# One decode step of attention and MLP on one core: wo in five chunks, buffers on lines of 512 bytes, eight unread matmuls

## The chip, the cores and the metric

The kernel runs on one core of one Trainium2 chip. Its time is device microseconds of one execution, as the median over several runs; the profile is one further execution, recorded by the hardware profiler. Of the core, the text speaks of PE (TensorE, the matmuls; PEld is its weight load), DVE (VectorE), ACT (ScalarE), POOL (GpSimd), SP (the queue that issues most transfers) and the 16 DMA engines that carry them. SBUF is the on-chip memory of 128 partitions, PSUM the accumulators that PE writes.

## The reference

One token goes through two branches that are added to it: attention over the last 4,096 positions of a cache with 4 key/value heads for 32 query heads, and a two-layer MLP. All arrays are bfloat16; D = 1024, F = 3584, head size 128.

```
xn = layernorm(x)
q  = (xn @ wq)                          # 1024 x 4096, 32 heads of 128
s  = q . k_cache[:, -4096:] / sqrt(128) # 4 heads, each for 8 query heads
o  = softmax(s) . v_cache[:, -4096:]
a  = o @ wo                             # 4096 x 1024
h  = gelu(layernorm(xn) @ w1 + b1)      # 1024 x 3584
b  = h @ w2 + b2                        # 3584 x 1024
out = x + a + b
```

## The kernel before

Everything that is computed is a product of one row with a large matrix, so nearly all of the 39.85 MB read are weights and cache, each used once. SP issues them in one queue, in this order: wq in four chunks, K of heads 0 and 1, W1 in three chunks, K of heads 2 and 3, V of four heads, W2 in two chunks, wo in seven chunks. A chunk is a number of rows of 128 partitions' worth: one row of wq is 8 KB per partition, of W1 7 KB, of W2 and wo 2 KB (`WQ_CHUNKS`, `W1_CHUNKS`, `W2_CHUNKS`, `WO_CHUNKS`, lines 22 to 25). Each chunk has a semaphore that its landing raises.

SBUF has three large buffers, allocated one behind the other after the small ones: KV (64 KB per partition, K and V), W1 (56 KB) and WA (64 KB). WA holds wq and later W2; W1 later holds wo rows 0 to 27; the K part of KV later holds wo rows 28 to 31 (`WOX`) and the output row (`OUT`). Hence three waits in SP's queue: W2 is issued once wq is used up (`pe_q`), wo once W1 is used up (`pe_h`), and the wo rows that lie in KV once the scores are done (`pe_sc`, line 426).

PE works in program order. First the sums of the layer norm of x (`pe_sum1`, line 286) and of xn (`pe_sum2`, line 312), each a matmul with a matrix of ones, followed by small DVE steps in `moments` (line 253). Then a loop over the 8 rows of wq (line 336), the spreading of q over heads (line 355), a loop over the 8 rows of W1 (line 389), a loop over 4 K heads (line 406), for which DVE transposes each K head as it lands (`turn_k`, line 345). Then the maximum, the exponentials and their transpose for the softmax, 32 matmuls with V (line 505), 56 with W2 (line 538) and 62 with wo (lines 549 and 558). The W2 and wo products go to two accumulators, `ACC[0]` for output columns 0 to 511 and `ACC[1]` for 512 to 1023, which lie in different rows of two PSUM banks. In the wo loop PE waits for each chunk's semaphore, then does two matmuls for each of its rows; the last chunk's pair stands in a block of its own, `pe_last`, which is branched to.

At the end ACT copies `ACC[0]` and DVE `ACC[1]` to SBUF. ACT issues the transfer of its half itself; SP waits for DVE and issues the other.

At the start POOL fills constants: identity matrices, ones, selection masks, zeros for `XZ`, `YZ` and `LQ`. DVE derives `SELI`, `QMASK`, `REPL` and `SEL2` from the identities between its layer-norm steps. `XZ` and `YZ` are zero but for the normalized x and y in every 97th column; PE reads shifted windows of them as its stationary operand.

Of the kernel before, what the change touches and what calls it, by code (L numbers as in the profile page):

```python
# [4 lines left out]
dt = mybir.dt  # L5
ALU = mybir.AluOpType
ACTF = mybir.ActivationFunctionType
AX = mybir.AxisListType

D = 1024  # L10
# [8 lines left out]
FC = F // 128  # L19
KC = D // 128  # L20
NQ = HQ * DH
WQ_CHUNKS = [1, 3, 2, 2]
W1_CHUNKS = [4, 2, 2]
W2_CHUNKS = [14, 14]
WO_CHUNKS = [13, 9, 4, 2, 2, 1, 1]

# [19 lines left out]
def bass_parallel_sum__sliding_block_cached__mixer_channel_mlp__decode_kernel(  # L46
# [17 lines left out]
    INV_D = 1.0 / D  # L64
# [3 lines left out]
    pe, dve, act, pool, sp = nc.tensor, nc.vector, nc.scalar, nc.gpsimd, nc.sync  # L68
# [12 lines left out]
    s_out = [nc.alloc_semaphore(f"s_out{n}") for n in range(2)]  # L81

    PE = Track(nc, "S_PE")
    DVE = Track(nc, "S_DVE")
    ACT = Track(nc, "S_ACT")
    POOL = Track(nc, "S_POOL")

    def sb(name, shape, dtype):
        return nc.alloc_sbuf_tensor(name, shape, dtype)

    identb = sb("identb", [128, 128], dt.bfloat16)
    identf = sb("identf", [128, 128], dt.float32)
    onesf = sb("onesf", [128, 128], dt.float32)
    SELI = sb("SELI", [128, 32], dt.float32)
# [6 lines left out]
    SEL2 = sb("SEL2", [4, 2], dt.bfloat16)  # L101
    XTT = sb("XTT", [128, 256], dt.bfloat16)
    XT16 = sb("XT16", [128, 16], dt.float32)
    msx = sb("msx", [128, 8], dt.float32)
    XNT = sb("XNT", [128, 8], dt.float32)
    XNTb = sb("XNTb", [128, 8], dt.bfloat16)
    YT16 = sb("YT16", [128, 16], dt.float32)
    msy = sb("msy", [128, 8], dt.float32)
    EXPW = sb("EXPW", [128, 1], dt.float32)
    YTb = sb("YTb", [128, 8], dt.bfloat16)  # L110
    TT = sb("TT", [128, 1024], dt.float32)
    QMASK = sb("QMASK", [128, 4], dt.float32)
# [11 lines left out]
    XZ = PT[:, 0:9 * 97 - 1]  # L124
    YZ = sb("YZ", [128, 9 * 97 - 1], dt.bfloat16)
    SELB = sb("SELB", [8, 2 * 97], dt.bfloat16)
    SUMP = sb("SUMP", [128, 1], dt.float32)
# [4 lines left out]
    OH = sb("OH", [32, DH], dt.bfloat16)  # L132
    OP = sb("OP", [128, 32], dt.bfloat16)
    KV = sb("KV", [128, HKV * W + HKV * NBLK * DH], dt.bfloat16)
    KT = KV[:, 0:HKV * W]
    WOX = KV[:, 0:4 * D]
    OUT = KV[0:33, 4 * D:4 * D + 512]
    V = KV[:, HKV * W: HKV * W + HKV * NBLK * DH]
# [34 lines left out]
    r = 0  # L173
# [12 lines left out]
    def ahead_of_barrier(engine, n):  # L186
# [15 lines left out]
    act.dma_start(XB[2:4, :], b2_rows).then_inc(s_b2, 16)  # L202
    DVE.mark(dve.memset(PS[:, 0:4 * 512], 0.0))

# [5 lines left out]
        base=0, channel_multiplier=1))  # L210
    c_onesf = POOL.mark(pool.memset(onesf[:, :], 1.0))
    POOL.mark(pool.memset(identb[:, :], 0.0))
    pool.wait_ge(POOL.sem, POOL.cnt)
    c_identb = POOL.mark(pool.affine_select(
        out=identb[:, :], in_=identb[:, :],
        pattern=[[-1, 128]], compare_op=ALU.not_equal, fill=1.0,
        base=0, channel_multiplier=1))
    POOL.mark(pool.memset(SEL[:, :], 0.0))
    pool.wait_ge(POOL.sem, POOL.cnt)
# [18 lines left out]
        out=SELB[:, :].rearrange("r (n m) -> r n m", n=2), in_=SELB[:, :].rearrange("r (n m) -> r n m", n=2),  # L238
        pattern=[[-16, 2], [-1, 97]], compare_op=ALU.not_equal, fill=1.0, base=0, channel_multiplier=16))
    POOL.mark(pool.memset(XZ[:, :], 0.0))  # L240
    c_z = POOL.mark(pool.memset(YZ[:, :], 0.0))
# [8 lines left out]
    def dve_dep():  # L250
        dve.wait_ge(DVE.sem, DVE.cnt)

    def moments(ms, T16):

        n = DVE.mark(dve.tensor_reduce(
            out=ms[:, 0:2],
            in_=PS[:, 7 * 512: 7 * 512 + 16].rearrange("p (a k) -> p a k", a=2),
            axis=AX.X, op=ALU.add))
        dve_dep()
        DVE.mark(dve.tensor_scalar(out=ms[:, 2:4], in0=ms[:, 0:2],  # L260
                                   scalar1=INV_D, scalar2=None, op0=ALU.mult))
        dve_dep()
        DVE.mark(dve.tensor_tensor(out=ms[:, 4:5], in0=ms[:, 2:3], in1=ms[:, 2:3], op=ALU.mult))
        dve_dep()
        v = DVE.mark(dve.scalar_tensor_tensor(
            out=ms[:, 5:6], in0=ms[:, 3:4], scalar=EPS, in1=ms[:, 4:5],
            op0=ALU.add, op1=ALU.subtract))
        act.wait_ge(DVE.sem, v)
        a = ACT.mark(act.activation(out=ms[:, 6:7], in_=ms[:, 5:6], func=ACTF.Sqrt))
        dve.wait_ge(ACT.sem, a)  # L270
        DVE.mark(dve.reciprocal(out=ms[:, 7:8], in_=ms[:, 6:7]))
        dve_dep()
        return n
# [10 lines left out]
    pe.wait_ge(DVE.sem, d_xsq)  # L284
    pe.wait_ge(POOL.sem, c_onesf)
    pe_sum1 = PE.mark(pe.matmul(PS[:, 7 * 512: 7 * 512 + 16], lhsT=onesf[:, :], rhs=XT16[:, 0:16]))  # L286
    dve.wait_ge(POOL.sem, c_identf)
    DVE.mark(dve.tensor_reduce(out=SELI[:, :], in_=identf[:, :].rearrange("p (i c) -> p c i", i=4),
                               axis=AX.X, op=ALU.add))
    dve_dep()  # L290
    DVE.mark(dve.tensor_reduce(out=QMASK[:, :], in_=identf[:, :].rearrange("p (t c) -> p t c", t=4),
                               axis=AX.X, op=ALU.add))
    DVE.mark(dve.tensor_copy(REPL[:, :].rearrange("p (i c) -> p i c", i=4),
                                      SELI[:, :].unsqueeze(1).to_broadcast([128, 4, 32])))
    dve.wait_ge(POOL.sem, c_identb)
    DVE.mark(dve.tensor_tensor(out=SEL2[:, :], in0=identb[0:4, 0:2], in1=identb[0:4, 2:4], op=ALU.add))
    dve.wait_ge(PE.sem, pe_sum1)
    moments(msx, XT16)
    DVE.mark(dve.tensor_scalar(out=XNT[:, :], in0=XT16[:, 0:8],
                               scalar1=msx[:, 2:3], scalar2=msx[:, 7:8],  # L300
                               op0=ALU.subtract, op1=ALU.mult))
    dve_dep()
    d_xn = DVE.mark(dve.tensor_copy(XNTb[:, :], XNT[:, :]))
    dve_dep()
    dve.wait_ge(POOL.sem, c_z)
    d_xz = DVE.mark(dve.tensor_copy(XZ[:, 96:9 * 97 - 1:97], XNTb[:, :]))
    DVE.mark(dve.tensor_copy(YT16[:, 0:8], XNTb[:, :]))
    dve_dep()
    d_ysq = DVE.mark(dve.tensor_tensor(  # L309
        out=YT16[:, 8:16], in0=YT16[:, 0:8], in1=YT16[:, 0:8], op=ALU.mult))  # L310
    pe.wait_ge(DVE.sem, d_ysq)
    pe_sum2 = PE.mark(pe.matmul(PS[:, 7 * 512: 7 * 512 + 16], lhsT=onesf[:, :], rhs=YT16[:, 0:16]))  # L312
    dve.wait_ge(PE.sem, pe_sum2)
    moments(msy, YT16)
    act.wait_ge(ACT.sem, ACT.cnt)
    ACT.mark(act.activation(out=EXPW[:, 0:1], in_=msy[:, 6:7], func=ACTF.Exp))
    d_y = DVE.mark(dve.tensor_scalar(
        out=YTb[:, :], in0=YT16[:, 0:8], scalar1=msy[:, 2:3], scalar2=msy[:, 7:8],
        op0=ALU.subtract, op1=ALU.mult))
    dve_dep()  # L320
    d_yz = DVE.mark(dve.tensor_copy(YZ[:, 96:9 * 97 - 1:97], YTb[:, :]))
    d_zs = DVE.mark(dve.memset(PS[:, 4 * 512:6 * 512], 0.0))

# [33 lines left out]
    dve.wait_ge(PE.sem, pe_qx)  # L357
    dve.wait_ge(POOL.sem, c_lq)
    act.wait_ge(PE.sem, pe_qx)
# [38 lines left out]

    pe.wait_ge(DVE.sem, d_zs)
    k_blocks = KT.rearrange("p (g n b j a) -> p g n b j a", g=HKV, n=2, b=16, j=4, a=32)  # L400
# [19 lines left out]
    def wo_at(r, nr):  # L420
        return W1[:, r * D:(r + nr) * D] if r < FC else WOX[:, (r - FC) * D:(r - FC + nr) * D]

    j0 = 0
    for j, nj in enumerate(WO_CHUNKS):
        if j0 == FC:
            sp.wait_ge(PE.sem, pe_sc)
        sp.dma_start(wo_at(j0, nj), wo_pm[:, j0 * D:(j0 + nj) * D]).then_inc(s_wo[j], 16)  # L427
        j0 += nj
# [17 lines left out]
    pe_nmb = PE.mark(pe.matmul(  # L446
        PS[:, 7 * 512 + 128: 7 * 512 + 129], lhsT=MX4[0:1, :], rhs=onesf[0:1, 0:1]))
    dve.wait_ge(PE.sem, pe_nmb)
# [33 lines left out]

    pe.wait_ge(s_b2, 32)
    pe.wait_ge(DVE.sem, d_nmb)
    for n in range(2):
# [7 lines left out]
    dve_dep()  # L493
    dve.wait_ge(POOL.sem, c_mask)
    DVE.mark(dve.tensor_scalar(out=RM[:, :], in0=MASK[:, :], scalar1=REC[:, 0:1], scalar2=None, op0=ALU.mult))
# [49 lines left out]
    for j, nj in enumerate(WO_CHUNKS[:-1]):  # L545
        pe.wait_ge(s_wo[j], 16)
        for _ in range(nj):
            for n in range(2):
                pe.matmul(ACC[n], lhsT=OP[:, r:r + 1], rhs=wo_at(r, 1)[:, n * 512:(n + 1) * 512],  # L549
                          start=False, stop=False)  # L550
            r += 1
    with nc.body("pe_turn", valid_engines=TENSOR):
        pe.br("pe_last").branch_hint(hint)
# [16 lines left out]
    a_out = ACT.mark(act.activation(out=OUT[0:1, :], in_=ACC[0], func=ACTF.Copy))  # L570
    act.wait_ge(ACT.sem, a_out)
    act.dma_start(out_row[:, 0:512], OUT[0:1, :]).then_inc(s_out[0], 16)
    sp.wait_ge(DVE.sem, d_out)
    sp.dma_start(out_row[:, 512:1024], OUT[32:33, :]).then_inc(s_out[1], 16)
    act.wait_ge(s_out[0], 16)
    sp.wait_ge(s_out[1], 16)

# [29 lines left out]
```

## Time and profile before

| | |
|---|---|
| median of 9 runs | 99.38 us (99.29 to 99.58) |
| the profiled execution's own time | 99.36 us |
| its span | 98.1 us |
| PE busy | 68.2 us, 69% of the span |
| DVE busy | 37.1 us, 38% |
| ACT, POOL busy | 5.8 and 6.7 us |
| granted PE clock, mean | 0.896 |
| DMA | 39.89 MB, mean 407 GB/s |
| packets on SP's queue (q1) | 3,458 |

The page cuts the span into 40 equal slices of 2.45 us. A digit is the busy share in tenths, 9 for 90% or more; PEclk is the clock granted to PE in the same tenths. The chain lists what ended last, followed back from the last instruction. In groups and timelines a line gives start, duration, engine, source line, operation and operands; in brackets stands the idle time before it and what ended it. A row of busy time by stretch gives the stretch, its length, then busy microseconds and count of PE, PEld, DVE, ACT and POOL, then PE's clock, the DMA share and GB/s.

### The profile page before, as it was taken

To read this page: it belongs to the slowest core of one execution; us is meant where nothing else is said; L and a number is where in the kernel's file an instruction comes from. 1 tells how busy PE (TensorE), PEld (TensorE's weight loads), DVE (VectorE), ACT (ScalarE), POOL (GpSimd) and SP (SyncE) were. 2 spreads that over 40 slices of the span, in tenths; PEclk is the share of its full clock that TensorE was granted. 3 is DMA by queue.
4 is the path that set the end of the run, shared out by engine and by line. 5 is a ranking of instruction groups with operands and counts; after the bars stand their busy time and mean duration, and the time that the engine had idled before them with its cause. 6 is when DMAs were issued, how large, how long until landed. Compare 5 with 4: busy or idle time off the path is not lost.

```text
span 98.1 us, 1063 instructions
## 1 busy us (share of the span) xinstructions
PE 68.2 (69%) x330; PEld 32.3 (33%) x330; DVE 37.1 (38%) x57; ACT 5.8 (6%) x11; POOL 6.7 (7%) x19
## 2 busy tenths in 40 slices
PE   0002299999983049999999743199991999754991
PEld 0002255555541025666644311133431233211320
DVE  4308571000018999500999544970008000000002
ACT  0500060000002000000000004000000000000002
POOL 6893000000000000000000000000000000000000
PEclk9999999999999556999999999755899589997599
DMA  5999999999999999999999999989989998989950
GB/s 154 434 483 453 392 434 434 427 391 428 438 526 397 386 403 427 444 402 428 428 428 428 428 446 514 409 374 514 421 374 469 416 445 377 458 385 420 413 226 8
DMA packets 3494, 39.89 MB, mean 407 GB/s; under 512 B 402, under 2 KB 420, under 8 KB 932
## 3 DMA queue, kind: packets, MB, share of 16 engines
q1 hardware_dynamic: 3458, 39.85, 95.8%
q8 instruction: 1, 0.02, 0.1%
q10 hardware_dynamic: 34, 0.01, 0.1%
q14 instruction: 1, 0.01, 0.0%
HBM read 39.86 MB, written 0.00 MB: 406 GB/s over the span
## 4 chain that ended last, share of the span: by engine, by line
DMA 81%; DVE 10%; SPq 4%; PE 2%; issue 1%
DMA KV<-in_A_k_cache_dram 43%; DMA KV<-in_A_wo_dram 38%; DVE KV L345 9%; PE PS L406 2%; SPq L176 1%; SPq L160 1%; SPq L166 1%; SPq L427 1%; DVE KV L568 1%; PE PS L558 0%
## 5 line engine op out<-in xcount | busy, mean ns | idle before, releaser
L345 DVE STREAM_TRANSPOSE KV<-KV 128x4096 bf16<-128x4096 bf16 x4 | 17.5, 4424 | 6.0 <-DMA KV<-in_A_k_cache_dram 5.9
L336 PE MATMUL PS<-WA,PT 128*97 x64 | 16.8, 433 | 0.1
L389 PE MATMUL PS<-W,YZ 128*97 x64 | 13.8, 379 | 4.2 <-POOLq L248 4.2
L389 PEld LDWEIGHTS PS<-W,YZ 128*97 x64 | 8.5, 133 | 9.4 <-issue 5.9
L336 PEld LDWEIGHTS PS<-WA,PT 128*97 x64 | 9.1, 143 | 7.4 <-issue 2.8
L549 PE MATMUL PS<-W,OP 128*1 128x512 bf16 x56 | 8.1, 452 | 3.0 <-DMA W<-in_A_wo_dram 3.0
L505 PE MATMUL PS<-KV,PT 128*32 128x512 bf16 x32 | 9.8, 481 | 0.1
L568 DVE CAST KV<-PS 1x512 bf16<-1x512 f32 x1 | 0.7, 683 | 20.1 <-PE PS L558 20.1
L538 PE MATMUL PS<-WA,GT 128*1 128x512 bf16 x56 | 7.9, 452 | 0.0
L406 PE MATMUL PS<-KV,LQ 128*128 x32 | 7.2, 380 | 0.5 <-DVE KV L345 0.5
L348 DVE STREAM_TRANSPOSE TT<-PS 128x1024 f32<-128x1024 f32 x1 | 1.2, 1250 | 14.1 <-PE PS L336 14.1
L286 PE MATMUL PS<-XT,onesf 128*128 128x16 f32 x2 | 0.6, 386 | 8.5 <-DVE XT L282 8.5
L505 PEld LDWEIGHTS PS<-KV,PT 128*32 128x32 bf16 x32 | 3.7, 117 | 5.8 <-issue 3.8
L549 PEld LDWEIGHTS PS<-W,OP 128*1 128x1 bf16 x56 | 2.7, 96 | 8.3 <-issue 3.5
L406 PEld LDWEIGHTS PS<-KV,LQ 128*128 x32 | 3.1, 98 | 4.5 <-issue 1.6
L538 PEld LDWEIGHTS PS<-WA,GT 128*1 128x1 bf16 x56 | 2.7, 96 | 4.7 <-issue 2.3
L510 DVE TENSOR_TENSOR TT<-PS,RM 32x512 f32<-32x512 f32 x1 | 0.7, 678 | 7.1 <-PE PS L505 7.1
L286 PEld LDWEIGHTS PS<-XT,onesf 128*128 128x128 f32 x2 | 0.5, 313 | 8.5 <-DVE XT L282 8.5
L452 ACT ACTIVATE Pe<-PS,NMB 128x512 bf16<-128x512 f32 x2 | 1.3, 683 | 28.4 <-DVE NMB L449 28.4
L570 ACT ACTIVATE KV<-PS 1x512 bf16<-1x512 f32 x1 | 0.6, 586 | 30.8 <-PE PS L558 30.8
L312 PE MATMUL PS<-YT,onesf 128*128 128x16 f32 x2 | 0.6, 384 | 2.4 <-DVE YT L309 2.4
L277 DVE STREAM_TRANSPOSE XTT<-XR 128x256 bf16<-128x256 bf16 x1 | 0.6, 631 | 4.2 <-DMA XR<-in_A_x_dram 4.2
(92 smaller groups left out, 33.7 us busy)
## 6 DMA issues: line engine op xcount, KB each, us to landing
WA<-in_B_w_dram SPq DMA_DIRECT2D x2, 3584.0 KB, 40.6
WA<-in_A_wq_dram SPq DMA_DIRECT2D x2, 2048.0 KB, 17.9
KV<-in_A_k_cache_dram SPq DMA_DIRECT2D x4, 1024.0 KB, 32.8
KV<-in_A_v_cache_dram SPq DMA_DIRECT2D x4, 1024.0 KB, 37.1
W<-in_B_w_dram SPq DMA_DIRECT2D x1, 3584.0 KB, 32.3
W<-in_B_w_dram SPq DMA_DIRECT2D x2, 1792.0 KB, 37.9
W<-in_A_wo_dram SPq DMA_DIRECT2D x1, 3328.0 KB, 34.5
WA<-in_A_wq_dram SPq DMA_DIRECT2D x1, 3072.0 KB, 11.2
```

The costliest lines, as they stand in the source:

```text
L160: sp.dma_start(WA[:, a:b], wq_pm[:, a:b]).then_inc(s_wq[j], 16)
L286: pe_sum1 = PE.mark(pe.matmul(PS[:, 7 * 512: 7 * 512 + 16], lhsT=onesf[:, :], rhs=XT16[:, 0:16]))
L336: last = pe.matmul(PS[0:97, n * 512:(n + 1) * 512], lhsT=shifted(XZ, s)[:, bass.ds(k, 1), :], rhs=wq_rows[:, bass.ds(k, 1), s * 1024 + n * ...
L345: dve.transpose(out=KT[:, g * W:(g + 1) * W], in_=KT[:, g * W:(g + 1) * W]).then_inc(r_k, 1)
L348: DVE.mark(dve.transpose(out=TT[:, :], in_=PS[:, 0:1024]))
L389: last = pe.matmul(PS[0:97, (2 + n) * 512:(2 + n) * 512 + HW], lhsT=shifted(YZ, s)[:, bass.ds(k, 1), :], rhs=w1_rows[:, bass.ds(k, 1), c: ...
L406: last = pe.matmul(PS[:, (4 + n) * 512:(5 + n) * 512], lhsT=q_blocks[:, bass.ds(g, 1), j, :], rhs=k_blocks[:, bass.ds(g, 1), n, :, j, :], ...
L452: a_exp = ACT.mark(act.activation(out=Pe[:, n * 512:(n + 1) * 512], in_=PS[:, (4 + n) * 512:(5 + n) * 512], func=ACTF.Exp, scale=SCALE, bi ...
L505: last = pe.matmul(PS[0:32, 0:512].rearrange("p (g d) -> p g d", g=HKV), lhsT=PT[:, b * 32:(b + 1) * 32], rhs=Vb[:, b, :, :], start=(b == ...
L538: pe.matmul(ACC[n], lhsT=GT[:, c:c + 1], rhs=W2[:, c * D + n * 512: c * D + (n + 1) * 512], start=False, stop=False)
L549: pe.matmul(ACC[n], lhsT=OP[:, r:r + 1], rhs=wo_at(r, 1)[:, n * 512:(n + 1) * 512], start=False, stop=False)
L568: d_out = DVE.mark(dve.tensor_copy(OUT[32:33, :], ACC[1]))
```

## The change

- wo comes in five chunks of 15, 9, 5, 2 and 1 rows; the first 24 rows lie in W1, the last 8 in the K part of KV, behind the wait for the scores. wq comes in chunks of 1, 3 and 4 rows, W1 in four chunks of 2.
- A pad ahead of KV puts it, and with it W1 and WA, on an address that 512 divides.
- After the matmuls of the first wo chunk PE does 8 more, all with the same operands, into PSUM bank 2, whose contents nobody reads afterwards.
- The matrix of ones holds 1/D instead, so that `moments` needs no scaling step. `identb` goes; POOL makes `QMASK` and `SEL2` itself. The normalized x and y are written straight into `XZ` and `YZ`, without the copies in between. DVE's wait for the zero fill of `LQ` moves ahead of the normalized x, and two later waits go. One fill of six PSUM banks at the start takes the place of one of four and a later one of two.
- SP issues the half of the output that ACT copies, ACT the half that DVE copies.

```diff
-WQ_CHUNKS = [1, 3, 2, 2]
-W1_CHUNKS = [4, 2, 2]
+WQ_CHUNKS = [1, 3, 4]
+W1_CHUNKS = [2, 2, 2, 2]
 W2_CHUNKS = [14, 14]
-WO_CHUNKS = [13, 9, 4, 2, 2, 1, 1]
+WO_CHUNKS = [15, 9, 5, 2, 1]
+WO_IN_W1 = sum(WO_CHUNKS[:2])
...
+    XNTb = XZ[:, 96:9 * 97 - 1:97]
+    YTb = YZ[:, 96:9 * 97 - 1:97]
...
+    if nc.sbuf_base % 512:
+        sb("PAD", [128, 512 - nc.sbuf_base % 512], dt.uint8)
     KV = sb("KV", [128, HKV * W + HKV * NBLK * DH], dt.bfloat16)
     KT = KV[:, 0:HKV * W]
-    WOX = KV[:, 0:4 * D]
-    OUT = KV[0:33, 4 * D:4 * D + 512]
+    WOX = KV[:, 0:(32 - WO_IN_W1) * D]
+    OUT = KV[0:33, 12 * D:12 * D + 512]
...
-    DVE.mark(dve.memset(PS[:, 0:4 * 512], 0.0))
+    d_ps = DVE.mark(dve.memset(PS[:, 0:6 * 512], 0.0))
...
-    c_onesf = POOL.mark(pool.memset(onesf[:, :], 1.0))
-    POOL.mark(pool.memset(identb[:, :], 0.0))
+    c_meanf = POOL.mark(pool.memset(meanf[:, :], INV_D))
+    POOL.mark(pool.memset(QMASK[:, :], 1.0))
...
-        DVE.mark(dve.tensor_scalar(out=ms[:, 2:4], in0=ms[:, 0:2],
-                                   scalar1=INV_D, scalar2=None, op0=ALU.mult))
...
-    DVE.mark(dve.tensor_scalar(out=XNT[:, :], in0=XT16[:, 0:8],
-                               scalar1=msx[:, 2:3], scalar2=msx[:, 7:8],
-                               op0=ALU.subtract, op1=ALU.mult))
-    dve_dep()
-    d_xn = DVE.mark(dve.tensor_copy(XNTb[:, :], XNT[:, :]))
-    dve_dep()
-    dve.wait_ge(POOL.sem, c_z)
-    d_xz = DVE.mark(dve.tensor_copy(XZ[:, 96:9 * 97 - 1:97], XNTb[:, :]))
-    DVE.mark(dve.tensor_copy(YT16[:, 0:8], XNTb[:, :]))
+    dve.wait_ge(POOL.sem, c_lq)
+    d_xz = DVE.mark(dve.tensor_scalar(out=XNTb, in0=XT16[:, 0:8],
+                                      scalar1=msx[:, 2:3], scalar2=msx[:, 7:8],
+                                      op0=ALU.subtract, op1=ALU.mult))
+    dve_dep()
+    DVE.mark(dve.tensor_copy(YT16[:, 0:8], XNTb))
...
-    d_zs = DVE.mark(dve.memset(PS[:, 4 * 512:6 * 512], 0.0))
...
     for j, nj in enumerate(WO_CHUNKS):
-        if j0 == FC:
+        if j0 == WO_IN_W1:
             sp.wait_ge(PE.sem, pe_sc)
...
                 pe.matmul(ACC[n], lhsT=OP[:, r:r + 1], rhs=wo_at(r, 1)[:, n * 512:(n + 1) * 512],
                           start=False, stop=False)
             r += 1
+        if j == 0:
+            for _ in range(8):
+                pe.matmul(PS[0:1, 2 * 512: 3 * 512], lhsT=OP[:, 0:1], rhs=wo_at(0, 1)[:, 0:512], start=True, stop=True)
...
-    act.wait_ge(ACT.sem, a_out)
-    act.dma_start(out_row[:, 0:512], OUT[0:1, :]).then_inc(s_out[0], 16)
-    sp.wait_ge(DVE.sem, d_out)
-    sp.dma_start(out_row[:, 512:1024], OUT[32:33, :]).then_inc(s_out[1], 16)
+    sp.wait_ge(ACT.sem, a_out)
+    sp.dma_start(out_row[:, 0:512], OUT[0:1, :]).then_inc(s_out[0], 16)
+    act.wait_ge(DVE.sem, d_out)
+    act.dma_start(out_row[:, 512:1024], OUT[32:33, :]).then_inc(s_out[1], 16)
```

## The prediction

> **What bounds the kernel now.** I read the page's chain of work first, then its slices, then the end of the chain in order of time, the timeline of the last 14 us, and busy time by stretch. The chain and the slices:
>
> ```profile
> ## 4 chain that ended last, share of the span: by engine, by line
> DMA 81%; DVE 10%; SPq 4%; PE 2%; issue 1%
> ...
> PEclk9999999999999556999999999755899589997599
> DMA  5999999999999999999999999989989998989950
> ```
>
> See that the DMA engines are full from the first slice to the 38th, while PE's granted clock falls to half several times. In the packet records, data runs from 1.04 to 95.37 us, 94.3 us, and a mean engine is busy for 94.2 us. So the transfers' rate sets the end; PE, DVE and ACT only have to keep up. The last part of the chain:
>
> ```profile
> 58.16 37.54 DMA KV<-in_A_wo_dram
> 95.70 0.04 issue
> 95.75 0.40 PE PS L558 x2
> 96.17 0.68 DVE KV L568
> ```
>
> After the last wo byte lands at 95.70 there remain one pair of matmuls, a copy to SBUF and the output's transfer, to 98.1. The profiled run took 99.36 us: span 98.1 plus 1.26 outside. The median of nine runs, 99.38, is 0.02 above it. The timeline shows PE against the wo chunks and the output's two issues:
>
> ```profile
> 75.78 7.89 PE L538 MATMUL PS<-WA,GT 128*1 128x512 bf16 x56
> ...
> 84.25 2.97 PE L549 MATMUL PS<-W,OP 128*1 128x512 bf16 x26 [0.57 <-DMA W<-in_A_wo_dram]
> ...
> 89.61 5.09 PE L549 MATMUL PS<-W,OP 128*1 128x512 bf16 x30 [2.39 <-DMA W<-in_A_wo_dram]
> ...
> 96.17 0.59 ACT L570 ACTIVATE KV<-PS 1x512 bf16<-1x512 f32 x1 [30.79 <-PE PS L558]
> ...
> 96.78 0.25 ACTq L572 DMA_DIRECT2D out_dram<-KV  x1
> 96.88 0.32 SPq L574 DMA_DIRECT2D out_dram<-KV  x1
> ```
>
> PE waits for chunk 0 (0.57 us) and chunk 1 (2.39 us), and still has nothing left over when the last row lands. A row is a pair of matmuls that start 4 to 7 ns apart in two column groups; rows follow each other every 0.216 us at full clock (84.25 to 86.84) and every 0.427 us at half clock (89.92 to 92.91). Busy time in stretches of 3.41 us, laid where the clock changes; the first figures are length and PE busy, PEclk stands near the end:
>
> ```profile
> 28.26:31.67 3.41, 1.57 (x7) 0.51 (x5) 2.15 (x4) 0.54 (x2) 0.00 (x0) 1.00 1.04 437
> 55.57:58.98 3.41, 1.99 (x9) 0.70 (x8) 1.29 (x2) 0.00 (x0) 0.00 (x0) 1.00 1.09 462
> 86.29:89.70 3.41, 1.02 (x12) 0.27 (x8) 0.00 (x0) 0.00 (x0) 0.00 (x0) 1.00 0.95 404
> 89.70:93.12 3.42, 3.42 (x18) 1.08 (x16) 0.00 (x0) 0.00 (x0) 0.00 (x0) 0.50 1.00 413
> ```
>
> Stretches busy 46% and 30% were followed by half clock, one busy 58% was not.
>
> **Alignment.** Nothing changes. As built, KV starts at byte 38,912, which is 76 x 512. The change drops identb (256 bytes) and XNT, XNTb, YTb (32 each as placed), 352 in all, to 38,560, and the pad of 352 puts KV back at 38,912; W1 and WA, behind it, are whole multiples of 512 long. 0 us. What a line off 512 costs no row shows, and the sum does not need it.
>
> **DMA count.** On SP's queue wq goes from 4 transfers to 3, W1 from 3 to 4, wo from 7 to 5: two fewer, the same bytes. One transfer is 128 packets, 8 on each of 16 engines, one per partition row, and one 4-byte packet per engine for the semaphore. Median packets take 84 ns at 2,048 bytes and 1,062 at 28,672: 27.2 bytes per ns and 8.8 ns that do not depend on size (8,192 should then be 310; it is 309). Packets stand back to back, so 2 x 8 x 8.8 = 141 ns and 2 x 9 ns are saved on every engine: **-0.16**. Bounds: the 28,672-byte packets of W1's first chunk had 16 of 128 slow, by some 100 ns each, about 0.1 us per engine; its successors of 14,336 bytes had one of 256. Split, that tenth may go: -0.26. Rows of 32,768 (wq) and 30,720 (wo) bytes are in no trace; if they are slow as W1's were, one packet in eight, each of the two chunks costs 0.1 us: +0.04. I take -0.16, by the medians.
>
> The Trainium skill, "DMA: Bandwidth & Descriptors" (section "Anatomy of one DMA"), gives each DMA a fixed cost of about 2 us (fitted for DMAs from GpSimd). If that were exposed, two fewer would be worth 4 us; the full engines show it overlapped, and the sum uses the packets.
>
> **Loads of constants and the layer norms.** Hidden. POOL loses identb's fill and select (0.19 + 0.29) and gains two small fills (0.09 each) and four selects (0.18 each) with their waits of 0.1: its last fill ends near 8.7 instead of 8.11. The new wait on c_lq ahead of the normalized x queues the rest of DVE behind it, but DVE gets there only near 10.3. DVE's fill of PSUM grows by half, 1.76 to 2.65, ending near 4.2; x lands at 7.42. The later fill (L322, 0.91) goes, off the path. Ahead of the x result go L260, L303 and L306 (0.17 to 0.19 each, with 0.03 between) and L291/L296's remainder: 0.7 us, so PE starts wq near 11.6, not 12.27.
>
> **wq in 1, 3, 4.** Rows 4 to 7 are now there at 21.75 rather than 16.89. From 11.6, 15 matmuls at 0.427 (to 18.0) and 17 at 0.216 bring PE to row 4 at 21.7: no wait. pe_q is at most 0.7 us earlier, never later by more than 0.1; SP waits for it (L416) to issue W2, with V queued until 58.7. 0 us.
>
> **W1 in twos; the wo issues.** The first W1 rows land near 31 instead of 35.47, so PE fills an idle stretch, ends W1 earlier and may wait before the fourth K group, whose transpose on DVE ends at 55.2 regardless. If that wait halves the clock, the group's 8 matmuls take 3.4 instead of 1.9 us, and the softmax, PV and W2 end up to 1.5 us later. Eight wo rows (4 before) now lie in KV behind pe_sc (57.3): those three issues are made 32 us before their bytes move, and all earlier ones are ahead of them. 0 us on the DMA side.
>
> **Chunks of 15, 9, 5, 2, 1, and the 8 matmuls.** wo landings before: 13 rows 84.11, 22 rows 89.56, 28 rows 93.22, 30 rows 94.44, 31 rows 95.05, 32 rows 95.70; about 0.61 us a row. After: 15 rows 85.32, 24 rows 90.77, 29 rows 93.73, 31 rows 94.89, 32 rows 95.54 (less what the dropped transfers save by then). PE at full clock: chunk 0 from 85.4, 15 x 0.216 = 3.24, to 88.64. The 8 matmuls lie in one column group, so 8 x 0.216 = 1.73 us, to 90.37: inside the wait for chunk 1, 0.40 us to spare. Chunk 1 from 90.82 to 92.76, chunk 2 from 93.78 to 94.86, chunk 3 from 94.94 to 95.37, the last at 95.59. So **0 us**, for PE never holds the end. Late W2 work has the 1.7 us between 83.67 and 85.4, then 0.40, then the 1.0 us ahead of chunk 2. Bounds: 0 below, since the last row's pair cannot start before it lands; above, the third rival.
>
> The row says that a wait of 2.39 us, 30% busy in its stretch, halved the clock. The Trainium skill, "TensorE: Matmul & The Clock Gate" (section "Part 1: The HAM clock gate"), has the clock drop after an idle window of about 3.4 us and advises against idle gaps longer than that. By that rule the wait of 2.1 us that chunk 1 would leave needs no filler, and the 8 matmuls can only delay; by the row they keep 15 + 9 rows in one warm stretch. The sum is the same by both, as they fit in the wait.
>
> **The output.** Before, ACT issues its own half at 96.785 (landed 97.90, 1.115 later), and SP the DVE half at 96.881 (landed 98.08, 1.199 later). Crossed: SP at 96.785 lands at 97.98, ACT at 96.881 at 98.00. **-0.08** at the end of the span. If the longer time belongs to the half and not to the queue, 0; the other bound is -0.10.
>
> **Sum.** 99.36 - 0.16 - 0.08 = 99.12, and I forecast 99.12 us (0.26% under the median). Bounds of its terms: 99.36 - 0.26 - 0.10 = 99.00 to 99.36 + 0.04 = 99.40.
>
> **The rivals.** *The packets saved do not pay.* An engine decides alone: of the last chunk's 16 landings, 15 lie between 94.71 and 95.23, and one at 95.70. At 77.9 us that engine's 26,624-byte packet took 1,518 ns instead of 987, beside an instruction fetch of 8,192 bytes. If such a straggler moves as it likes, 0.16 is lost in it, and the change is worth the output's crossing or nothing: 99.28 to 99.40. Against: the nine runs lie within 0.29 us.
>
> *The fetch changes.* PE's program grows by 16 instructions. A second fetch on the same engine would cost another 0.3 (its own 309 ns) to 0.53: 99.4 to 99.65. Without the fetch the end would be at 95.23: 98.65. For no change: the added instructions come after the point of the fetch.
>
> *Slower: PE falls to half clock in the last chunks.* Rows 24 to 30 have from 93.78 to 95.54, 1.76 us, and need 7 x 0.216 = 1.51; at half clock 7 x 0.427 = 2.99, and the last pair is late by 1.2 us, itself 0.2 longer: 99.12 + 1.4 = 100.5. It decides as soon as more than one of these seven rows is at half clock. If chunk 0 itself starts cold and W2 ends late too, the 8 matmuls take 3.4 us and push the same rows. For it: the waits before chunk 0 (1.7 us of 3.41, so 50% busy at worst, between the 46% that fell and the 58% that held) and chunk 2 (1.0). Against: the filler, and a half-clock chunk 0 costs only some 1.7 us before the clock returns, which 0.40 + 1.0 of waits nearly take.
>
> **How the numbers follow.** Forecast 0.60, its own range 99.00 to 99.30; saving lost 0.16 (99.28 to 99.40); more fetches 0.04; fetch gone 0.04; half clock 0.16, from 99.5 to 100.5. A change of 0.2%, 0.2 us, is about what a measurement of this kernel can tell from none: 99.18 and 99.58 are the limits. Faster: 0.54 of the forecast's 0.60 and the 0.04 = 0.58. Same: 0.06 + 0.16 = 0.22. Slower: 0.16 and 0.04 = 0.20. The range from 98.85 to 99.90 leaves out the fetch that goes and most of the half clock, some 0.15.
>
> **What would show it.** Right: q1 with some 288 packets fewer; the last landing near 95.5; full clock from chunk 0 on; waits of PE ahead of chunks 1, 2 and the last; SP and ACT halves landing within 0.1 us of each other. Wrong: half clock after 85 us; the last pair starting behind a matmul instead of a landing; a second instruction fetch before 95 us; a DMA slice under 9 in the middle.

## The result, and the profile after

The changed kernel takes 100.23 us (median of 10 runs, 100.06 to 101.26) against 99.34 for the kernel before (30 runs): a ratio of 1.0102, 95% interval 1.0085 to 1.0118. (The ratios, here and below, are not quotients of the medians beside them; they weigh all runs.) By the medians it is slower by 0.9 us, where 0.26% faster was forecast, and above the range given, 98.85 to 99.90. The profiled execution took 100.13 us, of which 98.7 are span.

The chain and the slices of its page:

```profile
## 4 chain that ended last, share of the span: by engine, by line
DMA 79%; DVE 10%; PE 5%; SPq 4%; issue 1%
...
PEclk9999999999999589999999855555999589999999
DMA  5999999999999999999999999899899999998920
```

Transfers still set the end, and PE's clock is full from chunk 0 on, as forecast. The timeline of the last 13 us of the changed kernel (start, duration, engine, line, operation; idle before and its end in brackets):

```profile
86.14 3.40 PE L548 MATMUL PS<-W,OP 128*1 128x512 bf16 x30 [1.70 <-DMA W<-in_A_wo_dram]
89.37 1.89 PE L554 MATMUL PS<-W,OP 128*1 128x512 bf16 x8
91.49 2.11 PE L548 MATMUL PS<-W,OP 128*1 128x512 bf16 x18 [0.22 <-DMA W<-in_A_wo_dram]
94.55 1.81 PE L548 MATMUL PS<-KV,OP 128*1 128x512 bf16 x14 [0.95 <-DMA KV<-in_A_wo_dram]
96.35 0.38 PE L561 MATMUL PS<-KV,OP 128*1 128x512 bf16 x2
...
97.39 0.32 SPq L575 DMA_DIRECT2D out_dram<-KV  x1
97.49 0.25 ACTq L577 DMA_DIRECT2D out_dram<-KV  x1
```

The filler, as the 8 unread matmuls are called from here on (L554), lies where it was put, inside the wait for chunk 1, and PE waits for chunks 0, 1 and 2. But all of it is 0.7 to 0.8 us later than worked out, beginning with chunk 0: 86.14 instead of 85.4. The last row, due at 95.54, landed at 96.31. The time was lost in a transfer before PE had done any filler. Each wo chunk has 16 landings, one per DMA engine, and they tell where:

```
last wo chunk      first    15th     16th landing (us)
before             94.71    95.23    95.70
after              94.58    95.08    96.31
```

Fifteen engines are 0.15 us earlier than before. One is 1.23 us behind them, where it was 0.47 behind before. What that engine carried besides is in the page's list of queues, first of the kernel before, then of the changed one:

```profile
q1 hardware_dynamic: 3458, 39.85, 95.8%
q8 instruction: 1, 0.02, 0.1%
q10 hardware_dynamic: 34, 0.01, 0.1%
q14 instruction: 1, 0.01, 0.0%
```

```profile
q1 hardware_dynamic: 3170, 39.85, 95.0%
q8 instruction: 2, 0.03, 0.1%
q10 hardware_dynamic: 34, 0.01, 0.1%
```

The 288 packets that were to go are gone from q1. The two queues called instruction carry code. Within the span, both kernels fetch 16,384 bytes on q8 after PE's last matmul. Before, there was one more fetch, of 8,192 bytes on q14 at 77.9 us. After, that one is missing, and there is a second of 16,384 bytes on q8 instead, at 80.73 us. It lasted 921 ns, and a wo packet of 30,720 bytes that began as it ended, at 81.63, took 1,645 ns where the others took 1,138. In the kernel before it was the same: the packet of 1,518 ns began as the shorter fetch ended, at 78.21, and not at 77.9, where the prediction put it. The packed trace does not say which DMA engine a packet used; that fetch, slow packet and late landing belong to one engine rests on there being one of each. So the question for the experiments was which part of the change lengthens the fetch, and which removes the other.

### The profile page after: what moved, and what is told of

Same layout as the page of the kernel before. It is cut to its first block, busy times and chain, and to the rows that moved or that the text cites. A ratio compares the mean times of both kernels' runs of the same rounds, so it can differ in the third digit from the quotient of the medians.

```text
span 98.7 us, 1072 instructions
## 1 busy us (share of the span) xinstructions
PE 69.0 (70%) x338; PEld 32.0 (32%) x338; DVE 36.5 (37%) x49; ACT 5.8 (6%) x11; POOL 7.1 (7%) x23
## 4 chain that ended last, share of the span: by engine, by line
DMA 79%; DVE 10%; PE 5%; SPq 4%; issue 1%
DMA KV<-in_A_k_cache_dram 42%; DMA KV<-in_A_wo_dram 37%; DVE KV L344 9%; PE PS L403 3%; SPq L178 2%; PE PS L548 2%; SPq L168 1%; SPq L162 1%; DVE KV L571 1%; PE PS L561 0%
## 5 line engine op out<-in xcount | busy, mean ns | idle before, releaser
L335 PE MATMUL PS<-WA,PT 128*97 x64 | 15.5, 405 | 1.6 <-POOLq L260 1.5
L387 PE MATMUL PS<-W,YZ 128*97 x64 | 14.7, 387 | 1.3 <-POOLq L260 1.3
L335 PEld LDWEIGHTS PS<-WA,PT 128*97 x64 | 8.4, 132 | 8.3 <-issue 4.0
L403 PE MATMUL PS<-KV,LQ 128*128 x32 | 8.4, 422 | 2.3 <-DVE KV L344 2.3
L295 PE MATMUL PS<-XT,meanf 128*128 128x16 f32 x2 | 0.6, 386 | 9.0 <-DVE XT L291 9.0
L548 PE MATMUL PS<-W,OP 128*1 128x512 bf16 x48 | 5.5, 379 | 1.9 <-DMA W<-in_A_wo_dram 1.9
L548 PEld LDWEIGHTS PS<-W,OP 128*1 128x1 bf16 x48 | 2.0, 83 | 5.5 <-issue 2.2
L205 DVE MEMSET PS<- 128x3072 f32 x1 | 2.6, 2618 | 0.6 <-issue 0.6
L548 PE MATMUL PS<-KV,OP 128*1 128x512 bf16 x14 | 1.8, 378 | 1.0 <-DMA KV<-in_A_wo_dram 1.0
L430 DVE TENSOR_REDUCE MXP<-PS 128x1 f32<-128x1024 f32 x1 | 1.2, 1223 | 3.3 <-PE PS L403 3.3
## 6 DMA issues: line engine op xcount, KB each, us to landing
WA<-in_A_wq_dram SPq DMA_DIRECT2D x1, 3072.0 KB, 11.4
```

What stands on the lines that cost most here:

```text
L205: d_ps = DVE.mark(dve.memset(PS[:, 0:6 * 512], 0.0))
L335: last = pe.matmul(PS[0:97, n * 512:(n + 1) * 512], lhsT=shifted(XZ, s)[:, bass.ds(k, 1), :], rhs=wq_rows[:, bass.ds(k, 1), s * 1024 + n * ...
L387: last = pe.matmul(PS[0:97, (2 + n) * 512:(2 + n) * 512 + HW], lhsT=shifted(YZ, s)[:, bass.ds(k, 1), :], rhs=w1_rows[:, bass.ds(k, 1), c: ...
L403: last = pe.matmul(PS[:, (4 + n) * 512:(5 + n) * 512], lhsT=q_blocks[:, bass.ds(g, 1), j, :], rhs=k_blocks[:, bass.ds(g, 1), n, :, j, :], ...
```

## The experiments

The compiled programs have these lengths, in instructions: PE 452 before and 468 after (8 matmuls are 8 weight loads and 8 products), DVE 73 and 63, SP 38 and 36. All ratios are to the kernel before on the same chip.

**The filler left out of the changed kernel, and the filler alone added to the kernel before.**

```diff
-        if j == 0:
-            for _ in range(8):
-                pe.matmul(PS[0:1, 2 * 512: 3 * 512], lhsT=OP[:, 0:1], rhs=wo_at(0, 1)[:, 0:512], start=True, stop=True)
```

> The changed kernel without the 8 unread matmuls; PE's program is 16 instructions shorter, as long as before. Theory A (the 16 added instructions make PE fetch 16,384 bytes of code at about 80 us, and the DMA engine that carries them lands its part of wo 1.2 us behind the others): no such fetch, last landing at 95.1 to 95.6, time 98.9 to 99.4 us. Theory B (the chunk sizes, with rows of 30,720 bytes, make the late engine): last landing stays at 96.3 and the time at 100.0 to 100.4. Theory C (the filler keeps PE's clock): chunk 1 at half clock and the last pair behind a matmul, 0.5 to 1.4 us late, time 99.5 to 101, whatever is fetched.

Measured: 98.99 us, ratio 0.9951 (0.9925 to 0.9977), no code fetch ahead of PE's last matmul; all 16 landings of the last chunk lie between 94.52 and 95.23. Its queues, and PE from chunk 0 on:

```profile
q1 hardware_dynamic: 3170, 39.85, 96.2%
q8 instruction: 1, 0.02, 0.1%
q10 hardware_dynamic: 34, 0.01, 0.1%
```

```profile
84.96 4.94 PE L548 MATMUL PS<-W,OP 128*1 128x512 bf16 x30 [3.71 <-DMA W<-in_A_wo_dram]
90.36 2.11 PE L548 MATMUL PS<-W,OP 128*1 128x512 bf16 x18 [0.46 <-DMA W<-in_A_wo_dram]
93.44 1.84 PE L548 MATMUL PS<-KV,OP 128*1 128x512 bf16 x14 [0.96 <-DMA KV<-in_A_wo_dram]
95.28 0.38 PE L557 MATMUL PS<-KV,OP 128*1 128x512 bf16 x2
```

Chunk 0 ran in part at half clock (4.94 us instead of 3.40), and it did not matter: PE was still waiting for chunks 1 and 2. Theory B falls here, and theory C with it: chunk 1 ran at full clock without the filler, and the last pair started at its landing.

> The kernel before with nothing but the 8 unread matmuls added after its first wo chunk. Theory A: the fetch is of 16,384 bytes instead of 8,192, one engine lands 1.2 us instead of 0.5 behind, time 99.34 + 0.7 = 100.0, give or take 0.2. Theory B: as before, 99.3. Theory C: PE at full clock for the second chunk, time as before, 99.3, for PE did not hold the end.

The edit is the three lines above, put into the kernel before. Measured: 100.15 us, ratio 1.0062 (1.0036 to 1.0089). Its page has both fetches:

```profile
q8 instruction: 2, 0.03, 0.1%
q10 hardware_dynamic: 34, 0.01, 0.1%
q14 instruction: 1, 0.01, 0.0%
```

And two engines are late: the last chunk's landings end 95.11, 95.32, 95.85, 96.56. The 8,192 bytes account for a lag of 0.5 us, as in the kernel before; the 16,384 for 1.2, as in the changed one. PE waited for every chunk, so the filler's own work cost nothing. With it the second chunk kept the clock:

```profile
90.46 2.11 PE L549 MATMUL PS<-W,OP 128*1 128x512 bf16 x18 [0.67 <-DMA W<-in_A_wo_dram]
```

These 9 rows took 2.11 us at full clock, and the next two chunks 1.03 and 0.59. In the kernel before, the clock was at half from 89.70 to 93.11, and the three chunks took 5.09 us together. But PE does not hold the end, so the clock that was kept bought nothing.

**Is it the length of PE's program?** Two kernels keep all 8 matmuls and shorten PE's program elsewhere.

```diff
-    for b in range(NBLK):
+    for b in range(NBLK - 8):
...
-                         start=(b == 0), stop=(b == NBLK - 1))
+                         start=(b == 0), stop=(b == NBLK - 9))
```

> The changed kernel with its 8 unread matmuls, but the last 8 of the 32 matmuls with V left out, so that the output lacks a quarter of the cache; PE's program is again as long as before. Theory A by length of program: no 16 KB fetch, time 98.9 to 99.4. If the fetch belongs to the 8 matmuls themselves (their place, one column group, one bank) and not to the length: 100.0 to 100.4, with the fetch at about 79.

Measured: 99.59 us (98.73 to 100.31; 99.47 without the longest run, which the ratio leaves out), ratio 0.9992 (0.9955 to 1.0029). The fetch is gone, as theory A by length has it, and the last landing is 95.03. The median missed the 98.9 to 99.4 expected for a reason that the timeline shows:

```profile
84.77 6.11 PE L548 MATMUL PS<-W,OP 128*1 128x512 bf16 x30 [3.66 <-DMA W<-in_A_wo_dram]
90.71 1.46 PE L554 MATMUL PS<-W,OP 128*1 128x512 bf16 x6
...
95.89 0.38 PE L561 MATMUL PS<-KV,OP 128*1 128x512 bf16 x1
```

With W2 done early, PE waited 3.66 us, the clock fell, chunk 0 took 6.11 us, and the filler began at 90.71, when chunk 1 had landed (90.09). From there PE was behind to the end: a matmul of the last row starts at 95.89, 0.86 us after its landing. This is the prediction's slower rival in its main part: chunk 0 starts at half clock, and the filler behind it pushes the last rows. The rival had W2 end late as well; here W2 ends early, because work was left out.

```diff
-    for b in range(NBLK):
-        last = pe.matmul(PS[0:32, 0:512]..., start=(b == 0), stop=(b == NBLK - 1))
...
+    for b in range(8):
+        pe.matmul(PS[0:32, 0:512]..., start=(b == 0), stop=False, ...)
...
+    with nc.Fori(1, 4, 1, engines=TENSOR) as i:
+        for b in range(8):
+            last = pe.matmul(PS[0:32, 0:512]..., lhsT=p_rows[:, bass.ds(i, 1), b, :], ..., start=False, stop=(b == 7), ...)
...
```

Three dots stand for what is left out.

> The changed kernel with all its 8 unread matmuls and the whole computation, but 24 of the 32 matmuls with V in a loop of 3 rounds, so that PE's program is 450 instructions long instead of 468. Theory A (length): no 16 KB fetch, last landing of all engines near 95.1. What then remains over the kernel without filler (99.0) is the filler's own cost: nothing where chunk 0 runs at full clock (99.0), up to 1.3 us where W2 ends early, chunk 0 starts at half clock and the filler ends behind chunk 1's landing. Expected median 99.0 to 99.6, with a wider scatter than without filler. If the fetch is not a matter of length: 100.2.

Measured: 98.93 us (98.83 to 99.13), ratio 0.9949 (0.9929 to 0.9968); the kernel without filler, run beside it, 98.84. This kernel does everything that the changed one does. Its PE program is 450 long, its page shows one instruction packet on q8, and it is 1.3 us faster. Here too chunk 0 ran partly at half clock, and the filler ended after chunk 1's landing:

```profile
85.03 5.09 PE L555 MATMUL PS<-W,OP 128*1 128x512 bf16 x30 [2.30 <-DMA W<-in_A_wo_dram]
89.95 1.46 PE L561 MATMUL PS<-W,OP 128*1 128x512 bf16 x6
...
95.33 0.38 PE L568 MATMUL PS<-KV,OP 128*1 128x512 bf16 x2
```

but the last pair still starts at its landing, 95.29. So the 8 matmuls cost nothing measurable as work, and 1.3 us as code.

**How much code?** 4 and 2 unread matmuls (PE 460 and 456 long):

```diff
-            for _ in range(8):
+            for _ in range(4):
```

> The changed kernel with 4 unread matmuls instead of 8: PE's program is 8 instructions longer than before, not 16. Theory A says that a boundary is crossed somewhere between 0 and 16 instructions: either 100.0 to 100.4 with the 16 KB fetch or 98.9 to 99.4 without, nothing in between. If the cost grows with the filler's own work: half, 99.6 to 99.8.

Measured: 100.25 us, ratio 1.0077 (1.0049 to 1.0105). The fetch is there, 16,384 bytes at 79.4 us; two engines end at 95.71 and 96.14 behind 94.93. Four matmuls cost as much as eight. One of the two engines was late already before this fetch (76.24 against 75.49 at the end of W2). Two packets early in this trace were long, 1,449 ns at 4.7 us and 1,412 ns at 11.4, by 0.73 us together against the others of their sizes; that would account for it, if both went to this engine, which the trace does not say.

> The changed kernel with 2 unread matmuls: PE's program is 456 instructions long; with 452 there was no 16 KB fetch, with 460 there was. Theory by length says all or nothing: 98.9 or 100.2.

Measured: 99.60 us (99.21 to 99.89, four runs), ratio 1.0014 (0.9987 to 1.0040). Neither of the two values expected. No fetch delays wo: the last landing is 95.11 and the span 97.5, as without filler. But the time beyond the span is 2.05 us on average instead of 1.4. By span the boundary lies between 456 and 460 instructions. That the extra 0.6 us beyond the span is again a fetch, now in what follows the kernel, would fit, but the trace ends before it: that stays open.

**Which part removed the 8,192 bytes?** In the kernel before, they start 1.8 us after DVE's last instruction ahead of its final wait. The kernel without filler, with DVE's program made 73 long again:

```diff
     d_ps = DVE.mark(dve.memset(PS[:, 0:6 * 512], 0.0))
+    SPARE = sb("SPARE", [32, 16], dt.float32)
+    for i in range(10):
+        DVE.mark(dve.memset(SPARE[:, i:i + 1], 0.0))
```

> No filler, and 10 one-column fills of an unused buffer early on DVE, in its idle stretch before x lands, so that DVE's program is again 73 instructions long, as before, instead of 63. The kernel before fetched 8,192 bytes of code at 77.9 us, 1.8 us after DVE's last instruction ahead of its final wait; no kernel with the shorter DVE program did. Theory: DVE's length brings that fetch back, one engine lands 0.5 us behind, time 99.3 to 99.5. Rival: the fetch came from something else (SP's queue, 38 instructions against 36, or the chunks): no fetch, 99.0.

Measured: 99.64 us, ratio 1.0023 (1.0010 to 1.0035), 0.7 to 0.8 us slower than the same kernel without these ten fills, twice on the same chip (98.84 and 98.94). Its queues:

```profile
q8 instruction: 1, 0.02, 0.1%
q10 hardware_dynamic: 34, 0.01, 0.1%
q14 instruction: 1, 0.01, 0.0%
```

The fetch is back, at 77.61 us, and the last chunk's landings end 95.37 and 96.02: one engine 0.65 behind. Ten tiny instructions in an idle stretch at 4 us cost more than any of the edits was meant to gain. Some 0.25 of it is in all engines, which are that much later already at the end of W2 (first landing 75.20 against 74.91 and 74.97). That part is not shown to come from the fills. In every profile some packets of W1 are slow. What they take beyond the median of their size, between 24 and 45 us, is 0.48 us per engine here. In the three profiles of the kernel without filler it is 0.17, 0.31 and 0.40, and their last landings lie in the same order, 95.03, 95.13 and 95.23.

**The output's crossing.** In the changed kernel each half of the output is issued from the other engine's queue. The run named uncrossed did not have the edit that its expectation speaks of: it is the kernel without filler, a third time.

> The kernel without filler once more, on the chip of the runs beside it: 98.9 to 99.1, ratio 0.995 to the kernel before.

> No filler, and the output issued as before (ACT its own half, SP the half of DVE). In all kernels with the crossed output the time beyond the span was 1.39 to 1.50 us on average, with the old one 1.25 to 1.30; the span from the last landing to its end was 2.38 before and 2.39 after. Theory: the crossing gains nothing inside the span and costs 0.15 outside it; uncrossed, 0.15 us less than without filler alone, 98.85 if that is 99.0. Rival: the time beyond the span belongs to something else in the change: same as without filler, 99.0.

They measured 98.84 (0.9943, 0.9923 to 0.9963) and 98.94 (0.9954, 0.9938 to 0.9970), and say how well the kernel without filler repeats. The profile of the first says one thing more. There chunk 0 ran at full clock, as in the changed kernel, and nothing filled the wait for chunk 1 (two lines of its timeline, then its busy time by stretch):

```profile
84.77 3.40 PE L548 MATMUL PS<-W,OP 128*1 128x512 bf16 x30 [0.26 <-DMA W<-in_A_wo_dram]
90.14 2.11 PE L548 MATMUL PS<-W,OP 128*1 128x512 bf16 x18 [1.96 <-DMA W<-in_A_wo_dram]
86.89:90.31 3.42, 1.46 (x14) 0.44 (x12) 0.00 (x0) 0.00 (x0) 0.00 (x0) 1.00 0.93 399
90.31:93.72 3.41, 2.41 (x24) 0.83 (x22) 0.00 (x0) 0.00 (x0) 0.00 (x0) 1.00 0.98 408
```

PE waited 1.96 us, 43% busy in its stretch, and chunk 1 still ran at full clock, in 2.11 us. So in this profile the chunks of 15 and 9 rows did without the filler what it was added for. The run with the edit:

```diff
-    sp.wait_ge(ACT.sem, a_out)
-    sp.dma_start(out_row[:, 0:512], OUT[0:1, :]).then_inc(s_out[0], 16)
-    act.wait_ge(DVE.sem, d_out)
-    act.dma_start(out_row[:, 512:1024], OUT[32:33, :]).then_inc(s_out[1], 16)
+    act.wait_ge(ACT.sem, a_out)
+    act.dma_start(out_row[:, 0:512], OUT[0:1, :]).then_inc(s_out[0], 16)
+    sp.wait_ge(DVE.sem, d_out)
+    sp.dma_start(out_row[:, 512:1024], OUT[32:33, :]).then_inc(s_out[1], 16)
...
```

> No filler, and the output issued as before: ACT its own half, SP the half of DVE. (The run called uncrossed before this did not have that edit.) Kernels with the crossed output took 1.39 to 1.50 us beyond their span on average, those with the old one 1.25 to 1.30. Theory: crossing gains nothing inside the span and costs 0.15 outside: 98.75 where the kernel without filler took 98.84 to 98.99, and 1.25 to 1.30 beyond the span. Rival: the time beyond the span belongs to another part of the change: 98.9 and 1.42.

Measured: 98.76 us, ratio 0.9937 (0.9921 to 0.9952), the fastest of all. From the last landing (95.03) to the last half's landing (97.42) it took 2.39 us, as with the crossing (96.31 to 98.70) and before (95.70 to 98.08: 2.38). The time beyond the span is 1.22 us on average, against 1.40 to 1.50 in every crossed kernel but the one with 2 unread matmuls. So the crossing gains nothing in the span and costs 0.1 to 0.2 us beyond it. Why the end is longer where ACT's half lands last is not in the trace.

**The chunks.** The same kernel, with the chunk lists of before:

```diff
-WQ_CHUNKS = [1, 3, 4]
-W1_CHUNKS = [2, 2, 2, 2]
+WQ_CHUNKS = [1, 3, 2, 2]
+W1_CHUNKS = [4, 2, 2]
...
-WO_CHUNKS = [15, 9, 5, 2, 1]
-WO_IN_W1 = sum(WO_CHUNKS[:2])
+WO_CHUNKS = [13, 9, 4, 2, 2, 1, 1]
+WO_IN_W1 = sum(WO_CHUNKS[:4])
```

> As the run beside it (no filler, old output), and with the chunks of before for wq, W1 and wo too: what is left of the change is the shorter programs of DVE and POOL and the pad. Theory: the two transfers more cost 0.15, and DVE's fetch of 8,192 bytes is gone all the same, since SP's program is 38 long as before but DVE's is 63: 98.9, last landing 95.2. Rival: the chunks or SP's length decide over the fetch: 99.35, last landing 95.7.

Measured: 98.92 us, ratio 0.9947 (0.9931 to 0.9964). Two transfers more cost 0.16 us beside the run before it, by the medians. These runs hardly resolve so little: 0.09 of it is time beyond the span (1.31 us on average, 1.22 in the run before), and in the profiles, where the last landing is 0.40 later (95.43 against 95.03), 0.25 is slow packets of W1 (0.52 us per engine against 0.27). SP's program is 38 long here and there is no fetch of 8,192 bytes, so SP's length is not what brings it; and the shorter programs at the start alone, with everything else as before, are worth 0.43 us (99.35 to 98.92).

The medians together, in us, with the code fetched before wo has landed:

```
kernel                         PE    DVE   code fetched      15th, 16th landing   time
before                         452   73    8,192             95.23  95.70          99.34
after                          468   63    16,384            95.08  96.31         100.23
before + filler                468   73    8,192 + 16,384    95.85  96.56         100.15
after, 4 unread matmuls        460   63    16,384            95.71  96.14         100.25
after, no filler               452   63    none              95.23  95.23          98.99
  + 10 fills on DVE            452   73    8,192             95.37  96.02          99.64
after, V matmuls in a loop     450   65    none              94.96  95.29          98.93
  no filler, old output        452   63    none              94.97  95.03          98.76
  no filler, output, chunks    452   63    none              95.38  95.43          98.92
```

## Why the prediction was wrong, by its steps

**Alignment: 0.** Nothing contradicts it, since the addresses are the same. No run tried another address.

**DMA count: -0.16.** It agrees with what was measured, at the edge of what can be measured. The 15 undisturbed engines end 0.15 us earlier, and the old chunks cost 0.16 us by the medians; but three profiles of one kernel, the one without filler, differ by 0.20 in their last landing. The bound of -0.26 did not come, for W1 in chunks of two has slow packets too: 10 to 80 of the 512 of 14,336 bytes were more than 7% over their median in the ten profiles with these chunks. The unseen rows of 32,768 bytes took 1,213 ns, as the line through the other sizes gives; those of 30,720 took 1,138. None of 30,720 bytes but the one behind the fetch was slow.

**Loads of constants and the layer norms: hidden, 0.** Wrong, by omission. The durations were hidden, as worked out; the number of DVE's instructions was not. Ten fewer removed the fetch of 8,192 bytes, worth 0.43 us with the rest of the start. The step priced instructions by their time alone.

**wq in 1, 3, 4, and W1 in twos: 0 on the DMA side.** Right. PE did wait 1.5 us for wq's last chunk, where no wait was worked out, since its clock was full from 14.99 us instead of 18.02; nothing hung on it. The late scores came as described, in this profile: the fourth K group ran mostly at half clock (3.04 us, against 1.90 to 3.54 in the variants with the same chunks), SP made the last three wo issues at 58.43 instead of 57.32, and PE had the slack.

**The 8 matmuls: 0.** As work, right: 1.89 us in the wait for chunk 1, and 98.93 against 98.84 once their code was paid for elsewhere. Nor were they needed for the clock, in the one profile without them in which chunk 0 ran at full clock. As code, wrong by 1.2 to 1.3 us. This is the step that failed and turned the sign. The prediction saw the late engine and the fetch beside it, and dismissed a second one with "the added instructions come after the point of the fetch". Two things were wrong there. The fetch it had seen was not PE's but one that DVE's length decides over. And the fetch ran ahead of execution: 16,384 bytes were moved from 80.73 us on, when PE was at W2, 8.6 us before it reached the filler. The price given, 0.3 to 0.53, was that of 8,192 bytes; the lag of 16,384 measured 1.2. Its size follows from the packets: the fetch's own 921 ns and the 507 ns by which the next packet was longer make 1.43 us, of which 1.32 show as the lag at chunk 0 and 1.23 at the last chunk. For the 8,192 bytes they make 0.84 (309 and 531 ns), and the lag was 0.60 and 0.47.

On this, the Trainium skill has a rule that the prediction did not weigh: "Runtime: NRT & Kernel Launch" (section "Instruction fetch mechanics") says that instructions come in blocks of 16 KiB, 256 instructions, and that crossing into the next costs one step of a DMA queue, mostly hidden. The packets of 16,384 bytes agree with the size, those of 8,192 do not. The cost does not agree here: hidden from PE, yes, but not from the kernel, whose one late DMA engine holds the end by 1.2 us.

**The output: -0.08.** Wrong; the bound of 0 held inside the span. Crossed, ACT's half lands 1.21 us after its issue at 97.49 and SP's 1.13 after its own at 97.39. The longer time went with the half, or with the second issue, not with the queue. And the step did not look beyond the span, where the crossing costs 0.1 to 0.2.

**The rivals.** "The fetch changes", given 0.04 in each of its two forms, is what happened, in both at once: one fetch went and a larger one came. Its price was too low, 99.4 to 99.65 for 100.23, and it had the second fetch on the same engine, where the kernel with both has two late engines. A straggler that "moves as it likes", given 0.16, was not seen: in the kernels without a fetch ahead of the end the last landing is at most 0.33 us behind the one before it. The half clock, given 0.16, did not set the profiled run; it showed in the kernel with 24 of 32 V matmuls. The share of busy time on which its argument rests does not decide alone. A stretch that was 50% busy was followed by full clock in the changed kernel, here in its busy time by stretch (length, PE busy, then the others, PEclk near the end):

```profile
83.25:86.66 3.41, 1.71 (x18) 0.59 (x16) 0.00 (x0) 0.00 (x0) 0.00 (x0) 1.00 0.85 364
86.66:90.08 3.42, 3.42 (x32) 1.36 (x27) 0.00 (x0) 0.00 (x0) 0.00 (x0) 1.00 1.00 426
```

In the kernel with 4 unread matmuls another of 50%, from 30.11 us on, was followed by half clock, and the 43% above by full clock, where the prediction's row of 46% fell. In the profiles of all these kernels, stretches of 3.41 us at full clock, laid the same way, were followed by half clock where they were 38% busy or less and by full clock where they were 51% busy or more; between the two, both happened.

Added up from the runs: -0.43 for the shorter start, -0.16 for the chunks, +0.1 to +0.2 for the crossing, +1.2 to +1.3 for the filler's code, together 0.7 to 0.9 above 99.34; measured 0.9. These are differences along one chain of kernels, so that they add up proves nothing more than the experiments do.

## What to carry to other kernels

Where the DMA engines are full to the end, a kernel ends with the slowest of them: compare the last landing with the other fifteen before explaining anything else, and look in the same place for packets that are not data. Code is such a packet. An edit that adds or drops instructions, even instructions without use on an engine that is not the bound, should be counted against the lengths at which a fetch was seen to appear, here between 456 and 460 instructions on PE and between 65 and 73 on DVE; a loop bought 1.3 us here, more than any of the edits was meant to gain. Where the boundary lies in another program, these runs do not tell.

## What was not expected of the hardware

- A fetch of 8,192 bytes, 309 ns long by itself, put its DMA engine 0.5 to 0.65 us behind at the last chunk, and one of 16,384 bytes (921 ns) 1.2 us. In the kernel with both, two different engines were late, and in the 11 us from chunk 0's landing to the last their lag shrank by no more than 0.1 us.
- With ten fills of one column, done at 4 us in an idle stretch, the kernel took 0.7 to 0.8 us more, most of it (0.65, the late engine's lag) through code fetched at 77.6.
- The time beyond the span is no constant: 1.22 to 1.31 us with one order of the two output transfers, 1.40 to 1.50 with the other, 2.05 with a PE program of 456 instructions.
